# Packed attention and a two-layer sMeLU block on one core: values loaded ahead of queries, head groups by halves, the last output tile in two PSUM tiles, and other planner constants

## The chip, the cores and the metric

The kernel runs on one NeuronCore of a Trainium2 chip. Its time is the device time of one execution in microseconds (us); the figure given is the median over runs. The profile is of one execution and shows what each engine did: TensorE (PE, and PEld for its weight loads), VectorE (DVE), ScalarE (ACT), GpSimd (POOL) and SyncE (SP).

## The reference, cut to what matters

There are 8 batches, 8 heads, 576 tokens of 64 channels, and 32 packing queries per head. All inputs and the output are float32.

```python
p_packed = sm_attn(p, k, v)            # per batch and head: 32 x 64
out = sm_attn(q, p_packed, p_packed)   # 576 x 64
x = out.transpose(0, 2, 1, 3).reshape(8 * 576, 512)
h = x @ w_in                           # 512 -> 2048
g = where(h >= 1, h, where(h <= -1, 0, (h + 1)**2 / 4))
return g @ w_out                       # 2048 -> 512
```

## The kernel before, in words

**The work of a batch.** k and q of a batch are turned so that the channels lie on the partitions (`trans`, line 350): 12 PE transposes for each half of the heads into one PSUM tile, and then a copy to `kT` or `qT`. From batch 3 on (`TURNED`, line 19) DMA transposes on SP's queue do this instead (`turned`, line 485). `scores` (376) multiplies k by the packing queries, 12 matmuls and one exponential on ACT for each half i of the heads. `packed` (397) multiplies by v and sums; three small steps on ACT and DVE make `ppT`, the packed values of each head. The heads are in two groups g of four, and a group's 4 x 32 packed rows fill the 128 rows of a matmul: `weights` (432) makes scores of q against the packed values (`s2`), an exponential `eT`, its sums (`sm`), and by a logarithm and an exponential (`ln`, `rc`) the normalised weights `A`. `mk` (472) multiplies the packed values by a quarter f of w_in (`mp`), which a copy turns into `M`. Both `s2` and `mp` use PE in tiles of 64 rows by 32 columns, eight matmuls at a time; everything else uses the whole array.

**The two layers.** `hidden_tile` (512) makes one of 16 tiles of h of a batch from M and A (4 matmuls), then a first step on ACT, a second on ACT or DVE and a third on DVE, which writes `hT`. `out_tile` (555) sums 16 matmuls ("o-steps", one for each hidden tile) into a PSUM tile `o` for 128 tokens, nine tiles for two batches; then the tile is copied to SBUF (`ob`) and written by SP.

**What sets the order.** `Plan` (31 to 172) is a list scheduler that runs when the program is built. Each task has engines, a cost from the table `C` (line 12), a key and dependences. `choose` (71) takes for each engine the task that can start first, a lower key going ahead; copies that either ACT or DVE may do go to the one that ends sooner. Its order is then the fixed order of each engine's instructions. Until three `o` tiles have been taken it fills PE's idle time with matmuls on zeros (127 to 133 and 624), whose number is fixed by the plan too. PSUM holds three wide tiles ("W", `psW`) and two `o` tiles ("O"). `sc`, `tp`, `s2`, `sm`, `mp` and `h` all take a wide tile.

**Loads.** All loads that cast go through POOL's queue in the order of lines 285 to 299: k of batch 0 in two halves, q, v, then the quarters of w_in and w_out in turn, k, q and v of batch 1, and the rest of p. Loads of batch b + 2 wait until the buffers of batch b have been read (607 to 611). Out writes and DMA transposes stand in SP's queue in the plan's order.

**What the change touches:** the table `C` (12 to 16), `Plan.run` (138 to 142), the first loads (285 to 292), `trans` (366 to 374), `scores`, the head numbers in `packed`, `weights` and `mk`, the last tile in `out_tile` (570 to 585), and the order of keys (602).

Of the kernel before, what the change touches and what calls it, by code (L numbers as in the profile page):

```python
# [8 lines left out]

C = dict(load=3.0, w_in=2.65, w_out=2.55, out=9.0, p=3.1, land=1.9, xt=5.0, xland=2.5,
         tpp=0.06, tp=0.042, sc=0.034, pk=1.05, s2=0.25, sm=0.245, M=0.345, h=0.49, o=0.217, switch=0.05,
         pTc=0.1, Tca=1.12, Tcd=0.76, Tc2a=0.64, Tc2d=0.457, ex=0.82, ppT=0.42, ppo=0.41, ppa=0.4, ppd=0.2, rs=0.18, eT=0.74, ln=0.65, rc=0.68, A=0.82,
         Mca=1.0, Mcd=1.22, x=0.65, ta=0.683, td=0.457, hT=0.758, oba=0.585, obd=0.69,
         array=0.2, wake=2.0, tell=0.04, feed=0.1, slack=0.6, margin=0.15, wait=0.5)
NW, NO, NX, NB = 3, 2, 5, 6
# [13 lines left out]
class Plan:  # L31
# [77 lines left out]
    def run(self, idle):  # L109
# [11 lines left out]
        while n:  # L121
# [54 lines left out]
def kernel(  # L176
# [92 lines left out]

    L = {}  # L270

    def add_load(nm, b, parts=1, deps=()):
        for i, hs in enumerate([ALL] if parts == 1 else HS):
            L[nm, b, i] = add(DMA, C["load"] / parts, -1, deps, lambda nm=nm, b=b, hs=hs: load(nm, b, hs))
        if parts == 1:
            L[nm, b, 1] = L[nm, b, 0]

# [59 lines left out]

    K = {}

    def attention(b, key):  # L340

        kT, qT = lambda: kTs[b % 2], lambda: qTs[b % 2]
# [7 lines left out]
        def trans(nm, i, dst, prev):  # L350
            box, ky = {}, key[nm + "T" + str(i)]

            def mm():
                tp = box["tp"] = wide([P, X, 1024], bf16, "tp")
                for j in range(X):
                    for h2 in range(2):
                        for e in range(E):
                            o = (h2 * E + e) * TP
                            nc.tensor.transpose(tp[:, j, o:o + TP],  # L359
                                                tok[nm, b][:, 4 * i + 2 * j + h2, X * e:X * (e + 1)].rearrange("p c d -> p (c d)"),  # L360
                                                ident[:TP, :TP])
            split = 2 if b == 0 else 1
            t = add(PE, C["tp"] * 12, ky, [L[nm, b, i]] + prev, mm, takes="W", readers=split, mode=0)
            if split == 1:
                def cp(eng):
                    w = 4 * E * TP
                    copy(dst()[:, i, :w].rearrange("p (j c) -> p j c", j=X), box["tp"][:, :, :w // 2])(eng)
                return t, [both(cp, C["Tca"], C["Tcd"], ky, [t], frees=t)]
            res = []
            for j in range(X):  # L370
                def cp(eng, j=j):
                    w = 2 * E * TP
                    copy(dst()[:, i, j * w:(j + 1) * w], box["tp"][:, j, :w])(eng)
                res.append(both(cp, C["Tc2a"], C["Tc2d"], ky, [t], frees=t))
            return t, res

        def scores(i, deps):
            box, ky = {}, key["sc" + str(i)]

            def mm():  # L380
                sp = box["sp"] = wide([P, 2, FW], f32, "sp")
                for j in range(2):
                    for e in range(E):
                        for g in range(G):
                            h, o = G * (2 * i + j) + g, (e * G + g) * X * NP
                            w = ((G * j + g) * E + e) * TP
                            nc.tensor.matmul(sp[:, j, o:o + X * NP], kT()[:, i, w:w + P],  # L387
                                             pT[:, b, h].rearrange("p x n -> p (x n)"), start=True, stop=True)

            def ev(eng):  # L390
                nc.scalar.activation(ex().rearrange("p e g x a n -> p a (e g x) n")[:, 2 * i:2 * i + 2],  # L391
                                     box["sp"][:TP, :, :E * G * X * NP].rearrange("p j (c n) -> p j c n", n=NP),
                                     AF.Exp, scale=scale)
            t = add(PE, C["sc"] * 12, ky, deps, mm, takes="W", readers=1, mode=0)
            return t, add(ACT, C["ex"], ky, [t] + old("pk"), ev, frees=t)

        def packed(deps):
            box, ky = {}, key["pk"]

            def mm():  # L400
                pk = wide([P, 1024], f32, "pk")
                vt, ex_ = tok["v", b], ex()
                v_ = box["v"] = pk[:, :H * X * NP].rearrange("p (h y) -> p h y", h=H)
                for g in range(G):
                    for a in range(Q):
                        h = G * a + g
                        for e in range(E):
                            nc.tensor.matmul(v_[:, h].rearrange("p (x n) -> p x n", x=X),  # L408
                                             vt[:, h, X * e:X * (e + 1)].rearrange("p c d -> p (c d)"), ex_[:, e, g, :, a],
                                             start=(e == 0), stop=(e == E - 1))  # L410
# [21 lines left out]
        def weights(g, deps, r):  # L432
            box, ky, km = {}, key["s2" + str(g)], key["sm" + str(g)]

            def mm():
                s2 = box["s2"] = wide([P, X, FW], f32, "s2")
                for a in range(Q):
                    for x in range(X):
                        nc.tensor.matmul(s2[a * NP:(a + 1) * NP, x, :HALF], pp_of(x, G * a + g),  # L439
                                         qT()[x * D:(x + 1) * D, a // 2, (G * (a % 2) + g) * E * TP:][:, :E * TP], start=True, stop=True)  # L440

            def exp2(eng):
                box["eT"] = att.tile([P, X, HALF], bf16, tag="eT", name="eT")
# [28 lines left out]
        def mk(f, deps):  # L472
            box, ky = {}, key["M" + str(f)]

            def mm():
                mp = box["mp"] = wide([P, G, FW], f32, "mp")
                for a in range(Q):
                    for g in range(G):
                        nc.tensor.matmul(mp[a * NP:(a + 1) * NP, g], pp_of(g, G * a + g),  # L479
                                         w_in_sb[g * D:(g + 1) * D, a, f * FW:(f + 1) * FW], start=True, stop=True)  # L480
            t = add(PE, C["M"], ky, deps + [L["in", f]], mm, takes="W", readers=1, mode=2)
            return t, both(lambda eng: copy(M()[:, :, f * FW:(f + 1) * FW], box["mp"])(eng),
                           C["Mca"], C["Mcd"], ky, [t] + K.get((b - 2, "h"), []), frees=t)

        def turned(nm, i, dst, prev):
            def go():
# [68 lines left out]
    def out_tile(pr, i):  # L555
        box, prev = {}, []
        bs = range(2 * pr + i * P // S, 2 * pr + ((i + 1) * P - 1) // S + 1)

        def step(fi):
            if fi == 0:  # L560
                box["o"] = psO.tile([P, d_model], f32, tag="o", name="o")
            nc.tensor.matmul(box["o"], hT[:, fi, i * P:(i + 1) * P], w_out_sb[:, fi, :], start=(fi == 0), stop=(fi == KF - 1))  # L562

        def done(eng):
            box["ob"] = ops.tile([P, d_model], f32, tag="ob", name="ob")
# [3 lines left out]

        def done_last(eng):  # L570

            w = d_model // 2
            for j, (eng, queue) in enumerate(((ACT, nc.scalar), (DVE, nc.sync))):
                ob = ops.tile([P, w], f32, tag="ob" + str(j), name="ob" + str(j), bufs=1)
                copy(ob, box["o"][:, j * w:(j + 1) * w])(eng)
                for a, n, dst in out_rows(pr, i):
                    queue.dma_start(dst[:, j * w:(j + 1) * w], ob[a:a + n])
        for fi in range(KF):
            t = add(PE, C["o"], 100 + pr * NT + i, [wrote[b, fi] for b in bs] + prev + [L["out", fi // 4]],
                    lambda fi=fi: step(fi), mode=0, takes="O" if fi == 0 else None, readers=1, slack=C["slack"])  # L580
# [1 line left out]
            prev = [t]  # L582
            if fi == 0:
                owner = t
        both(done if 2 * pr + 2 < B or i + 1 < NT else done_last, C["oba"], C["obd"], b_key(pr, i), prev, frees=owner, takes="ob", holds=C["out"])

    def b_key(pr, i):
        return -0.5
# [66 lines left out]
```

## Time and profile before

| what | value |
|---|---|
| median of the runs | 260.59 us (259.56 to 261.15, 3 runs) |
| profiled execution | 259.97 us, of which its span is 258.1 us |
| PE busy | 248.6 us (96%) |
| ACT busy | 189.5 us (73%) |
| DVE busy | 176.1 us (68%) |
| DMA, mean | 133 GB/s, 34.38 MB |

An engine is busy while an instruction is in it. PE's matmuls overlap, so PE at 96% may still lose time; how far apart the starts of equal matmuls lie tells more. The profile's lines name an instruction by its line in the kernel, its engine and its tiles (out<-in). In the timeline a bracket gives the idle time before an instruction and what ended it. In the chain of waits the work that ended last is followed back in time.

### The profile page before, as it was taken

What the parts mean: (1) busy time and instruction counts of PE and PEld (TensorE: products, weight loads), DVE (VectorE), ACT (ScalarE), POOL (GpSimd) and SP (SyncE); (2) the same over time, 40 slices, a digit from 0 to 9 for tenths busy, and PEclk for the clock granted to TensorE, in tenths of its full rate; (3) what the DMA queues carried; (4) which work ended last, traced back from release to release, by engine and by line L of the source; (5) the groups of instructions that cost most, each with busy time, mean ns of one, the idle gap of its engine ahead of it and who ended that gap; (6) DMA issues with size and microseconds to landing.
All of it is one profiled execution on the core that took longest, in us unless ns stands there. A gap on an engine that the chain in (4) does not pass through costs nothing.

```text
span 258.1 us, 5590 instructions
## 1 busy us (share of the span) xinstructions
PE 248.6 (96%) x2273; PEld 145.2 (56%) x2273; DVE 176.1 (68%) x298; ACT 189.5 (73%) x304; POOL 27.4 (11%) x40
## 2 busy tenths in 40 slices
PE   7999999899999999999999999999999999999992
PEld 5977556357646645654655556555654465644440
DVE  5124997678899988999858885888367877940000
ACT  3438995789899799989869987998669885841110
POOL 8522312102101201110201000000000000000000
PEclk9999999999999999999999999999999999999998
DMA  7999999999999999999999994312021111132223
GB/s 100 181 207 207 206 205 194 218 228 209 164 177 165 164 218 195 166 156 144 181 138 159 214 221 89 79 30 54 4 80 41 43 41 42 43 81 82 60 64 83
DMA packets 54762, 34.38 MB, mean 133 GB/s; under 512 B 27472, under 2 KB 50256, under 8 KB 54736
## 3 DMA queue, kind: packets, MB, share of 16 engines
q0 software_dynamic: 24608, 18.55, 51.0%
q1 hardware_dynamic: 29968, 15.34, 33.8%
q8 instruction: 18, 0.29, 0.4%
q10 hardware_dynamic: 160, 0.13, 0.2%
q14 instruction: 8, 0.07, 0.1%
HBM read 37.22 MB, written 9.44 MB: 181 GB/s over the span
## 4 chain that ended last, share of the span: by engine, by line
PE 76%; DMA 15%; ACT 3%; POOL 2%; issue 1%; DVE 1%; POOLq 0%
PE o L562 45%; PE h L519 21%; DMA p_nat<-in_p_dram 8%; DMA w_out_sb<-in_moe_w_out_dram 7%; PE mp L479 3%; PE sp L387 2%; PE pk L408 2%; PE sm L449 1%; PE s L439 1%; ACT M L307 1%; PE tp L359 1%; PE pk L414 1%; ACT pT L307 1%; POOL w_in_sb L280 1%; ACT eT L444 1%
## 5 line engine op out<-in xcount | busy, mean ns | idle before, releaser
L562 PE MATMUL o<-w_out_sb,hT 128*128 128x512 bf16 x576 | 144.5, 379 | 0.7 <-ACT ob L307 0.5
L534 DVE SCALAR_TENSOR_TENSOR hT<-x 128x576 bf16<-128x576 f32 x128 | 93.3, 754 | 14.0 <-PE o L562 9.8
L562 PEld LDWEIGHTS <-hT 128*128 128x128 bf16 x576 | 54.5, 98 | 56.4 <-issue 5.0
L524 ACT ACTIVATE x<-h 128x576 f32<-128x576 f32 x128 | 78.4, 656 | 9.9 <-PE h L519 6.6
L519 PE MATMUL h<-A,M 128*128 128x288 bf16 x512 | 77.8, 286 | 0.3 <-ACT M L307 0.3
L519 PEld LDWEIGHTS <-M 128*128 128x128 bf16 x512 | 48.4, 98 | 24.7 <-issue 3.0
L529 DVE TENSOR_SCALAR x<-x 128x576 f32<-128x576 f32 x80 | 36.7, 459 | 16.9 <-ACT x L524 16.2
L307 ACT COPY ob<-o 128x512 f32<-128x512 f32 (+1 forms) x22 | 12.7, 577 | 30.8 <-PE o L562 30.7
L531 ACT ACTIVATE x<-x 128x576 f32<-128x576 f32 x48 | 32.1, 683 | 0.7
L307 DVE COPY ob<-o 128x512 f32<-128x512 f32 (+1 forms) x15 | 10.1, 673 | 26.6 <-ACT ob L307 24.9
L307 ACT CAST M<-mp 128x1024 bf16<-128x1024 f32 x20 | 19.9, 1008 | 1.2 <-PE mp L479 1.1
L624 PE MATMUL o<-zeros 128*128 128x256 bf16 x137 | 18.9, 285 | 1.2 <-DVE zeros L242 1.2
L307 DVE CAST M<-mp 128x1024 bf16<-128x1024 f32 x12 | 14.6, 1220 | 1.7 <-PE mp L479 1.6
L624 PEld LDWEIGHTS <-zeros 128*128 128x128 bf16 x137 | 13.4, 102 | 3.5 <-DVE zeros L242 1.2
L460 DVE SCALAR_TENSOR_TENSOR A<-eT,rs,rc 128x576 bf16<-128x576 bf16 x16 | 13.0, 814 | 2.7 <-ACT rc L457 2.6
L391 ACT ACTIVATE ex<-sp 96x768 bf16<-96x768 f32 x16 | 12.9, 814 | 2.0 <-PE sp L387 2.0
L254 POOL DMA_DIRECT2D k<-in_k_dram x9 | 7.3, 812 | 65.9 <-issue 28.0
L444 ACT ACTIVATE eT<-s,rs 128x576 bf16<-128x576 f32 x16 | 11.7, 743 | 2.9 <-PE s L439 2.8
L479 PE MATMUL mp<-w_in_sb,ppT 64*32 64x512 bf16 x256 | 13.1, 384 | 0.5 <-ACT x L524 0.5
L453 ACT ACTIVATE ln<-sm 128x576 f32<-128x576 f32 x16 | 10.5, 655 | 1.6 <-PE sm L449 1.4
L457 ACT ACTIVATE rc<-ln 128x576 f32<-128x576 f32 x16 | 10.9, 683 | 0.5
L387 PEld LDWEIGHTS <-kT 128*128 128x128 bf16 x192 | 7.8, 98 | 2.2 <-ACT kT L307 0.2
(47 smaller groups left out, 114.1 us busy)
## 6 DMA issues: line engine op xcount, KB each, us to landing
q<-in_q_dram POOLq DMA_DIRECT2D x8, 576.0 KB, 14.5
v<-in_v_dram POOLq DMA_DIRECT2D x8, 576.0 KB, 15.0
out_dram<-ob SPq DMA_DIRECT2D x23, 192.0 KB, 3.0
k<-in_k_dram POOLq DMA_DIRECT2D x7, 576.0 KB, 14.1
out_dram<-ob SPq DMA_DIRECT2D x24, 128.0 KB, 2.4
w_in_sb<-in_moe_w_in_dram POOLq DMA_DIRECT2D x4, 512.0 KB, 18.3
w_out_sb<-in_moe_w_out_dram POOLq DMA_DIRECT2D x4, 512.0 KB, 19.0
out_dram<-ob SPq DMA_DIRECT2D x23, 64.0 KB, 2.6
```

The source lines that it names most:

```text
L307: return lambda eng: nc.vector.tensor_copy(out_, in_) if eng == DVE else nc.scalar.copy(out_, in_)
L387: nc.tensor.matmul(sp[:, j, o:o + X * NP], kT()[:, i, w:w + P], pT[:, b, h].rearrange("p x n -> p (x n)"), start=True, stop=True)
L444: nc.scalar.activation(box["eT"], box["s2"][:, :, :HALF], AF.Exp, scale=rs()[:, g, 1:])
L460: nc.vector.scalar_tensor_tensor(A()[:, g], box["eT"], rs()[:, g, :1], box["rc"], ALU.mult, ALU.mult)
L479: nc.tensor.matmul(mp[a * NP:(a + 1) * NP, g], pp_of(g, G * a + g), w_in_sb[g * D:(g + 1) * D, a, f * FW:(f + 1) * FW], start=True, stop=True)
L519: nc.tensor.matmul(h[:, hf, :HALF], T[b, "M"][:, g, fi * P:(fi + 1) * P], T[b, "A"][:, g, hf], start=(g == 0), stop=(g == G - 1))
L524: nc.scalar.activation(box["x"], box["h"][:, :, :HALF], AF.Prelu, bias=-1.0, alpha=0.5)
L529: nc.vector.tensor_scalar(x, x, 1.0, 0.0, ALU.add, ALU.max)
L531: nc.scalar.activation(x, x, AF.Relu, bias=1.0)
L534: nc.vector.scalar_tensor_tensor(hT[:, fi, col:col + S].rearrange("p (a t) -> p a t", a=2), box["x"], 1.0, box["x"], ALU.min, ALU.mult)
L562: nc.tensor.matmul(box["o"], hT[:, fi, i * P:(i + 1) * P], w_out_sb[:, fi, :], start=(fi == 0), stop=(fi == KF - 1))
L624: plan.run(lambda: nc.tensor.matmul(o[:, :DW], zeros[:, :P], zeros[:, :DW], start=True, stop=True))
```

## The change

- The loads of batch 0 stand as k (two halves), v, q (two halves); before they stood as k (two halves), q, v.
- Head groups: `head(g, a) = 4 g + (a ^ g)`. Group 0 holds heads 0 to 3 and group 1 holds heads 5, 4, 7, 6; before, group g held the heads 2a + g. So `scores(i)` makes the exponentials of group i alone, and the `s2` of a group needs one half of qT alone. In `mk` the row half of PE is now that of the head's parity, no longer that of the group.
- `trans` copies a half of the heads in one piece for batch 0 too, on one engine; before, DVE and ACT copied half of it each.
- The first copy of M is DVE's.
- The last output tile sums its 512 columns as two of 256 in two PSUM tiles (the second a wide one), and each engine copies one; its larger rows are written first.
- The plan: `xland`, the landing of a DMA transpose after its issue, 6.0 for 2.5; a step of ACT or DVE of over 0.4 gives the engine back 0.085 sooner (`lap`); a switch of PE's mode is counted at 0.09 and only into the tiled mode (before 0.05, both ways); the first v and q are counted at 3.8 (`first`).

```diff
-         tpp=0.06, tp=0.042, sc=0.034, pk=1.05, s2=0.25, sm=0.245, M=0.345, h=0.49, o=0.217, switch=0.05,
+         tpp=0.06, tp=0.042, sc=0.034, pk=1.05, s2=0.25, sm=0.245, M=0.345, h=0.49, o=0.217, switch=0.09, lap=0.085, join=0.11,
...
-                cost += C["switch"]
+                cost += C["switch"] if t.mode else 0.0
...
-            self.now[e] = at + cost
+            self.now[e] = at + cost - (C["lap"] if e in ("ACT", "DVE") and cost > 0.4 else 0.0)
...
+        load("v", 0, ALL)
         make_identity(nc, ident)
...
-    add_load("q", 0)
-    add_load("v", 0)
+    L["v", 0, 0] = L["v", 0, 1] = add(DMA, C["first"], -1, (), lambda: None)
+    add_load("q", 0, 2, cost="first")
...
+    def head(g, a):
+        return 4 * g + (a ^ g)
...
-                sp = box["sp"] = wide([P, 2, FW], f32, "sp")
-                for j in range(2):
-                    for e in range(E):
-                        for g in range(G):
-                            h, o = G * (2 * i + j) + g, (e * G + g) * X * NP
-                            w = ((G * j + g) * E + e) * TP
-                            nc.tensor.matmul(sp[:, j, o:o + X * NP], kT()[:, i, w:w + P],
-                                             pT[:, b, h].rearrange("p x n -> p (x n)"), start=True, stop=True)
+                sp = wide([P, 1024], f32, "sp")
+                box["sp"] = sp[:TP, :E * X * Q * NP].rearrange("p (e y) -> p e y", e=E)
+                for e in range(E):
+                    o = sp[:, e * X * Q * NP:(e + 1) * X * Q * NP].rearrange("p (x a n) -> p x a n", x=X, a=Q)
+                    for a in range(Q):
+                        h = head(i, a)
+                        w = (h % 4 * E + e) * TP
+                        nc.tensor.matmul(o[:, :, a], kT()[:, i, w:w + P], pT[:, b, h], start=True, stop=True)
...
-                        nc.tensor.matmul(mp[a * NP:(a + 1) * NP, g], pp_of(g, G * a + g),
-                                         w_in_sb[g * D:(g + 1) * D, a, f * FW:(f + 1) * FW], start=True, stop=True)
+                        h = head(g, a)
+                        y = h % 2
+                        nc.tensor.matmul(mp[a * NP:(a + 1) * NP, g], pp_of(y, h),
+                                         w_in_sb[y * D:(y + 1) * D, h // 2, f * FW:(f + 1) * FW], start=True, stop=True)
...
+            if (b, f) == (0, 0):
+                return t, add(DVE, C["Mcd"], ky, [t], cp, frees=t)
...
-        ws = [weights(g, pc + qc0 + qc1, r) for g in range(G)]
+        ws = [weights(g, pc + (qc0, qc1)[g], r) for g in range(G)]
...
-            nc.tensor.matmul(box["o"], hT[:, fi, i * P:(i + 1) * P], w_out_sb[:, fi, :], start=(fi == 0), stop=(fi == KF - 1))
+            for o, cs in [(box["o"][:, :w], slice(w)), (box["o2"], slice(w, d_model))] if end else [(box["o"], slice(d_model))]:
+                nc.tensor.matmul(o, hT[:, fi, i * P:(i + 1) * P], w_out_sb[:, fi, cs], start=(fi == 0), stop=(fi == KF - 1))
...
-            for j, (eng, queue) in enumerate(((ACT, nc.scalar), (DVE, nc.sync))):
+            for j, (eng, queue, o) in enumerate(((ACT, nc.scalar, box["o"][:, :w]), (DVE, nc.sync, box["o2"]))):
...
-                copy(ob, box["o"][:, j * w:(j + 1) * w])(eng)
-                for a, n, dst in out_rows(pr, i):
+                copy(ob, o)(eng)
+                for a, n, dst in sorted(out_rows(pr, i), key=lambda x: -x[1]):
...
-    order = "kT0 qT0 kT1 sc0 qT1 sc1 pk s20 M0 s21 sm0 M1 sm1 M2 M3".split()
+    order = "kT0 kT1 sc0 qT0 sc1 qT1 pk s20 M0 s21 sm0 M1 sm1 M2 M3".split()
```

More of the change, by code (lines that the diff above doesn't have):

```diff
@@ L8 @@
 from concourse._compat import with_exitstack
-C = dict(load=3.0, w_in=2.65, w_out=2.55, out=9.0, p=3.1, land=1.9, xt=5.0, xland=2.5,
-         tpp=0.06, tp=0.042, sc=0.034, pk=1.05, s2=0.25, sm=0.245, M=0.345, h=0.49, o=0.217, switch=0.05,
-         pTc=0.1, Tca=1.12, Tcd=0.76, Tc2a=0.64, Tc2d=0.457, ex=0.82, ppT=0.42, ppo=0.41, ppa=0.4, ppd=0.2, rs=0.18, eT=0.74, ln=0.65, rc=0.68, A=0.82,
+C = dict(load=3.0, first=3.8, w_in=2.65, w_out=2.55, out=9.0, p=3.1, land=1.9, xt=5.0, xland=6.0,
+         tpp=0.06, tp=0.042, sc=0.034, pk=1.05, s2=0.25, sm=0.245, M=0.345, h=0.49, o=0.217, switch=0.09, lap=0.085, join=0.11,
+         pTc=0.1, Tca=1.12, Tcd=0.76, ex=0.82, ppT=0.42, ppo=0.41, ppa=0.4, ppd=0.2, rs=0.18, eT=0.74, ln=0.65, rc=0.68, A=0.82,
          Mca=1.0, Mcd=1.22, x=0.65, ta=0.683, td=0.457, hT=0.758, oba=0.585, obd=0.69,
@@ L361, in mm, with cp @@
                                                 ident[:TP, :TP])
[L362 to L375, printed above, removed]
+            t = add(PE, C["tp"] * 12, ky, [L[nm, b, i]] + prev, mm, takes="W", readers=1, mode=0)
+            def cp(eng):
+                w = 4 * E * TP
+                copy(dst()[:, i, :w].rearrange("p (j c) -> p j c", j=X), box["tp"][:, :, :w // 2])(eng)
+            return t, [both(cp, C["Tca"], C["Tcd"], ky, [t], frees=t)]
         def scores(i, deps):
@@ L557, in out_tile, with spare @@
         bs = range(2 * pr + i * P // S, 2 * pr + ((i + 1) * P - 1) // S + 1)
+        end = 2 * pr + 2 == B and i + 1 == NT
+        w = d_model // 2
+        def spare():
+            box["o2"] = wide([P, w], f32, "o2")
         def step(fi):
@@ L584, in out_tile @@
                 owner = t
-        both(done if 2 * pr + 2 < B or i + 1 < NT else done_last, C["oba"], C["obd"], b_key(pr, i), prev, frees=owner, takes="ob", holds=C["out"])
+        both(done_last if end else done, C["oba"], C["obd"], b_key(pr, i), prev, frees=owner, takes="ob", holds=C["out"])
     def b_key(pr, i):
```

23 lines of the change are left out of this document (12 added, 11 removed).

## The prediction

> **What bounds the kernel now.** I read the windows by stage first, then the chain of waits, then the timeline where PE is not full.
>
> ```profile
> span 258.1 us, 5590 instructions
> 0.00:23.60 23.60, 21.57 (x277) 17.70 (x277) 8.78 (x24) 10.18 (x16) 11.63 (x21) 1.00 1.11 170
> 23.60:82.00 58.40, 55.66 (x607) 33.39 (x600) 48.16 (x78) 50.65 (x80) 8.59 (x11) 1.00 1.33 198
> 82.00:223.60 141.60, 141.60 (x1262) 80.77 (x1260) 113.71 (x189) 120.48 (x195) 7.19 (x9) 1.00 0.76 116
> 223.81 29.58 PE o L562 x137
> 20.36 3.00 PE L624 MATMUL o<-zeros 128*128 128x256 bf16 x26
> ```
>
> The second number after the length is PE's busy time. From 82 to 223.6 us PE is never idle, and then 137 o-steps run at 29.58 / 137 = 0.216 us each; a tile of h takes 0.49 (a chain row below has eight h matmuls in 0.98). So after 82 us there is nothing to gain but at the very end: the change must win before 82 us, and what it puts off there costs in full. Before 23.6 us PE mostly turns zeros, (3.00 - 0.27) / 25 = 0.11 us each.
>
> ```profile
> 11.75 0.75 POOL L280 DMA_DIRECT2D w_in_sb<-in_moe_w_in_dram  x1 [2.42 <-DMA q<-in_q_dram]
> 15.63 0.87 PE L408 MATMUL pk<-ex,v 96*128 96x64 bf16 x24 [0.36 <-DMA v<-in_v_dram]
> 22.71 0.82 DVE L460 SCALAR_TENSOR_TENSOR A<-eT,rs,rc 128x576 bf16<-128x576 bf16 x1 [0.58 <-ACT rc L457]
> 23.64 1.15 PE L519 MATMUL h<-A,M 128*128 128x288 bf16 x8
> 26.04 0.65 PE L519 MATMUL h<-A,M 128*128 128x288 bf16 x4
> 33.10 0.11 PEld L479 LDWEIGHTS <-ppT 64*32 64x32 bf16 x8 [0.29 <-DMA w_in_sb<-in_moe_w_in_dram]
> 34.54 0.99 ACT L307 CAST M<-mp 128x1024 bf16<-128x1024 f32 x1
> 35.68 2.12 PE L519 MATMUL h<-A,M 128*128 128x288 bf16 x16
> 38.52 1.19 PE L359 MATMUL tp<-ident,k 96*128 96x96 bf16 x24 [0.50 <-DMA k<-in_k_dram]
> 44.36 0.87 PE L408 MATMUL pk<-ex,v 96*128 96x64 bf16 x24 [0.38 <-DMA v<-in_v_dram]
> 47.01 0.81 PE L562 MATMUL o<-w_out_sb,hT 128*128 128x512 bf16 x3 [0.46 <-ACT ob L307]
> 50.20 0.41 PE L449 MATMUL sm<-eT,onesblk 128*128 128x288 bf16 x2 [0.27 <-ACT pT L307]
> 55.47 0.65 PE L519 MATMUL h<-A,M 128*128 128x288 bf16 x4
> 76.94 0.41 PE L479 MATMUL mp<-w_in_sb,ppT 64*32 64x512 bf16 x8 [0.53 <-ACT x L524]
> 79.30 0.65 PE L519 MATMUL h<-A,M 128*128 128x288 bf16 x4 [0.27 <-ACT M L307]
> ```
>
> The third load is in SBUF by 11.7, the fourth by 15.6; batch 0's A waits for it and the first h runs at 23.64. But the stream of loads goes on: the last quarter of w_in stops PE at 33.1, k of batch 1 at 38.5, its v at 44.36. These loads keep their places. The brackets from 38.5 on sum to 0.50 + 0.38 + 0.46 + 0.27 + 0.53 + 0.27 = 2.4 us: about all that a better order could still find.
>
> **The change, part by part.** I walk through the order in which the changed program is built, each step beginning at the latest of its data, its engine and its PSUM tile, with these durations:
>
> ```profile
> L307 DVE COPY kT<-tp 128x1152 bf16<-128x1152 bf16 x2 | 1.4, 753 | 0.5 <-PE tp L359 0.5
> L307 ACT COPY kT<-tp 128x1152 bf16<-128x1152 bf16 x2 | 2.2, 1112 | 0.0
> L307 DVE COPY ob<-o 128x512 f32<-128x512 f32 x14 | 9.7, 691 | 1.7 <-PE o L562 1.2
> L453 ACT ACTIVATE ln<-sm 128x576 f32<-128x576 f32 x16 | 10.5, 655 | 1.6 <-PE sm L449 1.4
> L457 ACT ACTIVATE rc<-ln 128x576 f32<-128x576 f32 x16 | 10.9, 683 | 0.5
> 24.69 3.92 ACT L524 ACTIVATE x<-h 128x576 f32<-128x576 f32 x7
> 38.51 1.28 ACT L531 ACTIVATE x<-x 128x576 f32<-128x576 f32 x2
> ```
>
> *Loads, whole copies, groups by halves.* The copies of a half in batch 0 become one of 0.753 on DVE; they end before v lands either way, so this costs and gains nothing. v now lands third, by 11.7; pk stands behind 15 zeros, which end at 12.65, where it started at 15.63. The halves of q land at about 13.7 (halfway between the third and the fourth load) and 15.6. With 7 zeros, the transposes and a copy, qT's first half is ready at 15.9, and 11 zeros end at 16.1: s2 of group 0 runs at 16.2. Group 1 follows its half of q: transposes at 16.55, copy to 18.0, s2 at 18.25, its sm behind the first M block at 19.85; ln, rc and A (0.655 + 0.683 + 0.82, with the steps between) end at 22.5, and 24 zeros at 22.7. First h at 22.7: 0.9 us sooner.
>
> *What becomes of it by 44 us.* The second M block now stands behind three tiles of h, and its copy on ACT behind three first steps (3.92 / 7 = 0.56 each): it ends at 26.1, h tile 4 starts at 26.45 (before 26.04), and two o-steps more are done. The fourth M block comes after four h tiles and five o-steps, and its copy after two extra second steps on ACT (0.64 each): 35.3 to 36.3 (before 34.54 to 35.53). h tile 12 is at 36.45 (before 35.68) with three o-steps (0.65) more: all of the 0.9 is gone. Four o-steps then stand ahead of k's transposes: 39.45 (before 38.52). The first copy of kT falls to ACT, behind two second steps: 40.6 to 41.7, where DVE took 0.75 at once. The next o tile needs the first one's copy by DVE (0.691): 43.7 to 44.4. Six o-steps stand ahead of pk, so pk is at 45.8 (before 44.36), with 38 o-steps ahead of it instead of 30: 8 x 0.216 = 1.73 done for 1.44 us. Ahead by 0.3.
>
> *Batch 1's attention.*
>
> ```profile
> 47.77 0.79 ACT L307 COPY pT<-tpp 64x768 bf16<-64x768 bf16 x1 [0.39 <-DVE pT L307]
> 48.59 0.56 DVE L307 COPY pT<-tpp 64x768 bf16<-64x768 bf16 x1 [0.86 <-ACT pT L307]
> 49.35 0.79 ACT L307 COPY pT<-tpp 64x768 bf16<-64x768 bf16 x1
> 56.13 0.51 PE tp L359 x12
> ```
>
> The four copies from one PSUM tile go one after the other. Now three are ACT's: 3 x 0.79 + 0.55 from 47.35 end at 50.2 with the steps between. The s2 of group 1 takes their PSUM tile (the built addresses say so) and stops PE from 49.3 to 50.35. Both orders have 57 o-steps ahead of batch 1's first h. It comes at 56.65 (before 55.47), with one more group of transposes (0.51) done: behind by 0.7.
>
> *Batch 1's h, batch 2's attention.*
>
> ```profile
> 65.90:78.21 12.31, 11.77 (x135) 6.21 (x134) 11.18 (x20) 11.32 (x19) 0.77 (x1) 1.00 1.36 178
> 80.16 0.98 PE h L519 x8
> ```
>
> Here ACT is the limit (11.32 of 12.31 us), as the waits at 76.94 and 79.30 say. pk goes ahead of two h tiles, which leaves seven tiles and 19 o-steps to cover the chain of s2, sm and A instead of four and 15. But the second M copy of this batch moves from DVE to ACT, 1.0 us on the engine that is late. Step by step h tile 0 of batch 2 comes at 79.45 instead of 78.21, with the same work ahead (90 o-steps); some of the 1.2 comes back in the next waits: 1.1 us behind at 81.4.
>
> *After 82 us.* Earlier sc and pk mean fewer o-steps as cover: between batch 3's first h and batch 4's s2 stand 7 o-steps, where 23 stood. Each of the eleven tiles of h there asks 0.56 of ACT and 0.49 of PE, so ACT falls up to 11 x 0.07 = 0.8 behind. Bounds: 0 (no wait shows in this stage now) and 16 x 0.216 = 3.5 us (all of the lost cover missed); I take 0.4, near the lower, as half of those 0.8. DMA transposes:
>
> ```profile
> 62.66 5.89 SPq L487 DMA_TRANSPOSE qT<-q  x1
> ```
>
> Both of k now stand ahead of both of q on SP (before, q's first stood between), so sc's second half has its data one issue (5.89 us) sooner, while 20 o-steps fewer (4.3 us) stand ahead of it in batch 4. SP's outputs stand between them; I cost this at nothing, covered by that issue, and at up to 4 us if a write that waits for its copy holds it up. The plan's 6.0, lap and switch act through the order alone; both orders enter the tiled mode 40 times.
>
> *The end.*
>
> ```profile
> 253.41 0.37 ACT L307 COPY ob<-o 128x256 f32<-128x256 f32 x1 [2.82 <-PE o L562]
> 253.82 0.86 ACTq L577 DMA_DIRECT2D out_dram<-ob  x2
> 253.82 0.42 DVE L307 COPY ob<-o 128x256 f32<-128x256 f32 x1 [24.86 <-ACT ob L307]
> 254.27 0.82 SPq L577 DMA_DIRECT2D out_dram<-ob  x2
> ```
>
> DVE waited for ACT's copy from the same PSUM tile; from its own it starts 0.41 sooner. The larger write, issued second, ended last; issued first it goes half of 0.82 sooner, and the smaller one then ends last, which I estimate to leave 0.2 of that. Two matmuls of 256 columns cost 32 x 0.11 - 16 x 0.216 = 0.06. Together -0.6.
>
> *Sum:* +1.1 + 0.4 - 0.6 = +0.9 us on the profiled execution, which has 259.97 us (span 258.1 and 1.9 around it), 0.6 under the median. On the median: 260.59 + 0.9 = 261.5.
>
> **A row against a rule.** The M block of the changed kernel sends both row halves of PE into each of its two PSUM banks; before, each half had a bank.
>
> ```profile
> 52.38 0.34 PE mp L479 x8
> ```
>
> Eight matmuls of 512 columns take 0.34 us in all, one alone 0.216: they overlap. The Trainium skill (TensorEngine Tiling (Array Packing), Gotcha 1: PSUM Pressure) says that different row tiles cannot access one PSUM bank at the same time. By that rule the halves would take turns; no row here shows it, and the sum above takes nothing. [...]
>
> **The rivals.**
> 1. *Faster.* The plan's order holds better than my walk: the six waits of 2.4 us go, as they are what the new lap and the earlier pk address, and the end gives 0.6: 260.59 - 3.0 = 257.6, over 1% under. For it: seven tiles cover batch 2's chain. Against: ACT is full there. It decides if ACT, not PE, has idle time in 66 to 78 us.
> 2. *Slower by lost cover.* One mechanism, 82 to 130 us: with 16 o-steps fewer before batch 4's s2, PE stands while ACT catches up. It costs 3.5 us at most; with the rest, 260.59 + 1.1 + 3.5 - 0.6 = 264.6. It decides from about 2.1 us of waits there (263.2 in all). Against it: PE's row of 141.60 in 141.60 leaves room unseen.
> 3. *Slower by turns in a bank.* If the row halves take turns, each of 32 M blocks is two rounds, 0.216 more: +6.9, so 268.4. Nothing in before bears on it, as each half has its own bank there.
> 4. *It does nothing:* the sooner h is eaten by the loads, nothing else moves: 260.0. This lies within my forecast's own range.
>
> **How the numbers follow.** My walk (with rival 4): 0.60, own range 260.0 to 263.0; rival 1: 0.15; rival 2: 0.20; rival 3: 0.05. The range leaves out rival 3 and most of rival 1: 258.3 to 264.6. A change of under 1% (2.6 us) can hardly be told from none here: within it falls the walk, 0.60; faster 0.15; slower 0.20 + 0.05 = 0.25.
>
> **What would show it.** First h near 22.7; pk of batch 1 near 45.8; a wait of about 1 us of s2 for pT near 50; first h of batch 2 near 79.5; PE full from 82 on but for a few tenths; M blocks of 0.34; both last copies starting together. I am wrong if batch 2's first h comes before 78, if PE shows waits of over 1 us after 82, or if M blocks lengthen.

## The result and the profile after

The changed kernel takes 262.01 us (median of 9 runs, 261.55 to 264.05), the kernel before 259.74 (9 runs, 259.28 to 261.15): a ratio of 1.0102, 95% interval 1.0079 to 1.0125. The forecast was 261.5 against 260.59, a ratio of 1.0035; the time lies in its range. So much for the sum. The terms behind it are another matter: up to batch 2 the change gained 1.5 us where I had it losing, and behind that it lost about 3.4 us where I had it losing 0.4. (Three runs, one of the kernel before and two of kernels below, were over 1% longer at a granted clock of 0.946 to 0.993 and are left out.)

The windows of the profiled execution after, then the last of them for the kernel before and for the changed kernel without `lap` (the first experiment). The numbers in brackets are instructions; the second bracket counts weight loads, one for each matmul.

```profile
span 259.8 us, 5588 instructions
0.00:22.50 22.50, 20.90 (x266) 17.28 (x267) 10.06 (x24) 7.93 (x12) 11.81 (x22) 1.00 1.10 171
22.50:82.00 59.50, 56.16 (x621) 34.53 (x630) 47.02 (x81) 52.99 (x82) 10.07 (x12) 1.00 1.30 204
82.00:222.00 140.00, 137.75 (x1199) 77.62 (x1219) 105.11 (x186) 113.10 (x184) 6.35 (x8) 1.00 0.71 112
```

```profile
82.00:222.00 140.00, 140.00 (x1250) 79.56 (x1248) 112.22 (x186) 118.88 (x192) 7.19 (x9) 1.00 0.77 117
```

```profile
82.00:222.00 140.00, 138.39 (x1218) 79.90 (x1239) 114.31 (x187) 117.13 (x193) 6.64 (x8) 1.00 0.72 115
```

In the same 140 us PE began 1219 matmuls instead of 1248. (PE's busy time is no guide here: the two traces with 1199 and 1218 matmuls miss about 20 records each, which leaves holes in it; the loads are all there.) Which ones are missing is in the groups of weight loads by line in that stretch: M is the operand of h, hT that of an o-step, kT that of the scores. First before, then after.

```profile
L519 PEld LDWEIGHTS <-M 128*128 128x128 bf16 x355 | 33.7, 98 | 17.2 <-issue 1.3 <-PE s L439 1.0
L562 PEld LDWEIGHTS <-hT 128*128 128x128 bf16 x345 | 32.8, 98 | 31.3 <-issue 2.8
L387 PEld LDWEIGHTS <-kT 128*128 128x128 bf16 x108 | 4.4, 98 | 1.1
```

```profile
L522 PEld LDWEIGHTS <-M 128*128 128x128 bf16 x345 | 32.8, 97 | 18.2 <-issue 3.6
L572 PEld LDWEIGHTS <-hT 128*128 128x128 bf16 x338 | 32.2, 98 | 32.3 <-issue 4.0
L387 PEld LDWEIGHTS <-kT 128*128 128x128 bf16 x96 | 3.9, 98 | 0.9
```

A matmul of h is worth 0.49 / 4 = 0.1225 us, an o-step 0.216, one of the scores 0.03 (12 in 0.35). So 10 x 0.1225 + 7 x 0.216 + 12 x 0.03 = 3.1 us of work were not done. I call this the work lost behind 82 us; it is counted, not read from idle time.

PE's timeline of the kernel after, with the places that the forecast named, and ACT's at the one wait among them:

```profile
22.52 1.63 PE L522 MATMUL h<-A,M 128*128 128x288 bf16 x12
33.95 0.41 PE L479 MATMUL mp<-w_in_sb,ppT 64*32 64x512 bf16 x8
34.30 1.04 PE L572 MATMUL o<-w_out_sb,hT 128*128 128x512 bf16 x4
35.88 2.13 PE L522 MATMUL h<-A,M 128*128 128x288 bf16 x16 [0.55 <-ACT M L309]
45.08 0.86 PE L405 MATMUL pk<-ex,v 96*128 96x64 bf16 x24
49.72 0.32 PE L437 MATMUL s<-qT,ppT 64*32 64x288 bf16 x8 [1.60 <-ACT pT L309]
55.44 0.65 PE L522 MATMUL h<-A,M 128*128 128x288 bf16 x4
76.22 1.29 PE L522 MATMUL h<-A,M 128*128 128x288 bf16 x8
```

```profile
46.65 1.60 ACT L309 COPY pT<-tpp 64x768 bf16<-64x768 bf16 x2
48.87 0.79 ACT L309 COPY pT<-tpp 64x768 bf16<-64x768 bf16 x1 [0.62 <-DVE pT L309]
```

The first h is where I put it (22.52; forecast 22.7), and s2 of group 1 does wait for the copies of pT, for 1.60 us rather than the 1 forecast. But h tile 12 is at 35.88 (36.45), pk at 45.08 (45.8), batch 1's first h at 55.44 (56.65), and batch 2's first h is the second tile of the row at 76.22, so at 76.71 (79.45; before 78.21, with the same 90 o-steps ahead). The M block still takes 34.30 - 33.95 = 0.35 us.

The last copies of the kernel after:

```profile
255.30 0.37 ACT L309 COPY ob<-o 128x256 f32<-128x256 f32 x1 [2.75 <-PE o L572]
255.41 0.42 DVE L309 COPY ob<-o 128x256 f32<-128x256 f32 x1 [25.60 <-PE o L572]
255.71 0.86 ACTq L586 DMA_DIRECT2D out_dram<-ob  x2
255.86 0.79 SPq L586 DMA_DIRECT2D out_dram<-ob  x2
```

They start together, as the edit means them to. From the first copy to the end of the span it is 259.8 - 255.30 = 4.5 us, and was 258.1 - 253.41 = 4.7: the end is worth 0.2.

So the profiled pair, 259.8 - 258.1 = +1.7, is -1.5 by batch 2's first h, about +3.4 behind it (3.1 of it in the counted 140 us), and -0.2 at the end. Both executions start alike: the 28 zeros from 4.41 us on take 2.99 us in each, which matters below.

### The profile page after: what moved, and what is told of

Read it like the earlier page. It is cut to its first block, busy times and chain, and to the rows that moved or that the text cites. A ratio compares the mean times of both kernels' runs of the same rounds, so it can differ in the third digit from the quotient of the medians.

```text
span 259.8 us, 5588 instructions
## 1 busy us (share of the span) xinstructions
PE 248.0 (95%) x2253; PEld 146.3 (56%) x2287; DVE 170.2 (66%) x302; ACT 184.9 (71%) x296; POOL 28.2 (11%) x41
## 4 chain that ended last, share of the span: by engine, by line
PE 73%; ACT 15%; DVE 7%; issue 3%; ACTq 0%
PE o L572 38%; PE h L522 21%; ACT x L527 6%; PE o L635 5%; DVE hT L537 4%; PE mp L479 3%; ACT M L309 2%; ACT x L534 2%; PE sp L387 2%; ACT eT L442 2%; ACT ln L451 1%; PE s L437 1%; PE tp L366 1%; PE pk L405 1%; DVE x L532 1%
## 5 line engine op out<-in xcount | busy, mean ns | idle before, releaser
L572 PE MATMUL o<-w_out_sb,hT 128*128 128x512 bf16 (+1 forms) x558 | 133.1, 373 | 1.3 <-issue 0.5
L572 PEld LDWEIGHTS <-hT 128*128 128x128 bf16 x592 | 56.0, 98 | 55.9 <-issue 5.4
L532 DVE TENSOR_SCALAR x<-x 128x576 f32<-128x576 f32 x92 | 41.3, 457 | 12.3 <-ACT x L527 11.8
L309 ACT CAST M<-mp 128x1024 bf16<-128x1024 f32 x29 | 29.1, 1015 | 0.0
L534 ACT ACTIVATE x<-x 128x576 f32<-128x576 f32 x36 | 24.0, 685 | 0.6
L635 PE MATMUL o<-zeros 128*128 128x256 bf16 x135 | 18.2, 285 | 1.2 <-DVE zeros L243 1.2
L255 POOL DMA_DIRECT2D q<-in_q_dram x9 | 7.1, 794 | 30.3 <-DMA qT<-q 19.5
```

The lines of the kernel that those rows point to most:

```text
L255: nc.gpsimd.dma_start(tok[nm, b][:, hs].rearrange("p h c d -> p h (c d)"), SRC[nm][b, hs].rearrange("h (p c) d -> p h (c d)", c=NC))
L309: return lambda eng: nc.vector.tensor_copy(out_, in_) if eng == DVE else nc.scalar.copy(out_, in_)
L532: nc.vector.tensor_scalar(x, x, 1.0, 0.0, ALU.add, ALU.max)
L534: nc.scalar.activation(x, x, AF.Relu, bias=1.0)
L572: nc.tensor.matmul(o, hT[:, fi, i * P:(i + 1) * P], w_out_sb[:, fi, cs], start=(fi == 0), stop=(fi == KF - 1))
L635: plan.run(lambda: nc.tensor.matmul(o[:, :DW], zeros[:, :P], zeros[:, :DW], start=True, stop=True))
```

## The experiments

**Which part costs: the plan's credit, or the rest?** The first four kernels take the change apart. Without the credit alone:

```diff
-         ... switch=0.09, lap=0.085, join=0.11,
+         ... switch=0.09, lap=0.0, join=0.11,
```

> The changed kernel with lap 0 instead of 0.085, so that the plan again counts each ACT and DVE step in full. Theory A (the lap lets the plan set tiles of h so close that PE waits for ACT by some hundredths at each, 3.3 us in all after 82 us): the waits after 82 us fall back to about those of before, PE is full there, and the time comes to about 257.5 to 259, 3 to 4 under the changed kernel and 1 to 2 under before. Theory B (the groups by halves and the other structure cost the time after 82 us, whatever the plan counts): 261 to 262, as the changed kernel.

Measured: 256.9 us (256.75 to 257.81), against 259.94 for the kernel before on the same chip: ratio 0.9891 (0.9869 to 0.9914). One number in the plan, which changes no step but only the order of the steps and which of ACT and DVE does a copy, is worth 5.1 us, and without it the change is a gain of 3 us. The groups of loads from 82 to 222 us say where:

```profile
L522 PEld LDWEIGHTS <-M 128*128 128x128 bf16 x356 | 33.8, 98 | 18.5 <-issue 2.8 <-PE h L522 0.2
L572 PEld LDWEIGHTS <-hT 128*128 128x128 bf16 x347 | 33.0, 98 | 30.5 <-issue 2.5
L387 PEld LDWEIGHTS <-kT 128*128 128x128 bf16 x96 | 3.9, 98 | 0.8
```

11 matmuls of h and 9 o-steps more than after in the same time: 1.35 + 1.94 = 3.3 us. The rest of the 4.9 us between the spans (259.8 and 254.9), 1.6 us, was lost before 82. There the 1.60 us that s2 waits for the copies of pT are gone without the credit: PE's waits from 28 to 82 us sum to about 3.0 us after, 1.3 without the credit and 2.7 before.

The same with the other two numbers of the plan put back as well:

```diff
-         ... xt=5.0, xland=6.0,
+         ... xt=5.0, xland=2.5,
-         ... switch=0.09, lap=0.085
+         ... switch=0.05, lap=0.0
-                cost += C["switch"] if t.mode else 0.0
+                cost += C["switch"]
```

> The changed kernel with all planner constants as before (lap 0, landing 2.5, switch 0.05 both ways): loads, halves, whole copies, first M copy and last tile alone. Theory A: as with lap 0 alone, 257.5 to 259. Theory B: 261 to 262. Theory C (the later landing is needed now that scores are asked for sooner): a wait for DMA transposes of over 1 us shows on PE between 100 and 130 us, which lap 0 alone doesn't have.

Measured: 257.49 us (257.0 to 258.09), ratio 0.9904 (0.9884 to 0.9924). PE shows no wait for a DMA transpose between 100 and 130 us, so theory C falls. The landing time of the DMA transposes and the price of the switch do nothing that shows beside `lap`.

The credit alone, on the kernel before:

```diff
-            self.now[e] = at + cost
+            self.now[e] = at + cost - (C["lap"] if e in ("ACT", "DVE") and cost > 0.4 else 0.0)
```

> The kernel before with the lap of 0.085 alone. Theory A: it has 64 pairs of h tiles with nothing between them on PE, where before has 42 and the changed kernel 48; waits of PE for ACT after 82 us of 3 to 5 us, and a time of 262 to 264. Theory B: the lap does nothing by itself, 259.5 to 260.5.

Measured: 263.95 us (263.08 to 264.2), ratio 1.0144 (1.0122 to 1.0166): 4.0 us slower. So the credit costs with either structure, 4.0 on the old one and 5.1 on the new one, and the other parts gain 3.0 without it and 1.9 with it.

The end alone, on the kernel before (two PSUM tiles for the last tile, the larger write first):

```diff
-                copy(ob, box["o"][:, j * w:(j + 1) * w])(eng)
-                for a, n, dst in out_rows(pr, i):
+                copy(ob, o)(eng)
+                for a, n, dst in sorted(out_rows(pr, i), key=lambda x: -x[1]):
```

> The kernel before with the last output tile in two PSUM tiles and its larger rows first, nothing else; the order of the rest is the same. The forecast's term of the sum: both copies start together and the last landing is 0.5 to 0.6 sooner, 259.2. Rival: the writes' own time sets the end, whichever copy comes first, 259.7.

Measured: 259.88 us, ratio 0.9996 (0.9984 to 1.0009). The two copies do start together in this kernel's timeline:

```profile
253.76 0.37 ACT L307 COPY ob<-o 128x256 f32<-128x256 f32 x1 [2.75 <-PE o L569]
253.87 0.42 DVE L307 COPY ob<-o 128x256 f32<-128x256 f32 x1 [24.50 <-PE o L569]
```

From the first copy to the end of the span (258.2) it is 4.4 us, 0.3 less than before. The edit does what it says, and is worth half of the 0.6 forecast at most; the runs can't tell it from nothing.

**Where does the credit cost?** The next two kernels give it to one half of the time each; the condition is on the time at which the plan places the step.

```diff
-... (C["lap"] if e in ("ACT", "DVE") and cost > 0.4 else 0.0)
+... (C["lap"] if e in ("ACT", "DVE") and cost > 0.4 and at > 82.0 else 0.0)
```

> The changed kernel, but the plan takes the 0.085 us of overlap into account only for steps that it places after 82 us. Without it the kernel took 256.9, with it 262.0: 5.1 us. Theory A (the credit lets ACT look as fast as PE, so fewer o-steps stand between tiles of h and PE waits): the lost starts of PE are 2.0 us more before 82 (4.90 against 2.93) and 3.4 us more behind it (1.87 + 2.78 against 0.27 + 0.98), so this kernel takes 256.9 + 3.4 = 260.3, and shows PE waiting behind 82 as the changed kernel does. Rival B (what is lost behind 82 is only the wait that an earlier stage passes on): 257 to 257.5. Rival C (any other order is as bad as any, the differences are chance): somewhere between 257 and 262 without waits behind 82.

> The changed kernel, with the 0.085 us of overlap only for steps that the plan places up to 82 us. Theory A: it loses the 2.0 us before 82 alone, above all the wait of s2 for the PSUM tile of pT near 50 us, and shows PE full from 82 on: 256.9 + 2.0 = 258.9. Rival B (the early part is what matters): 261 to 262. Rival C (as for the kernel before this one): between 257 and 262.

The second has `at <= 82.0`. Measured: 260.91 us with the credit behind 82 alone (ratio 1.0039, 1.0023 to 1.0055), 259.03 with the credit before 82 alone (0.9974, 0.9951 to 0.9998). Expected were 260.3 and 258.9; rival C asked for no waits behind 82 in the first, and there they are. The loads from 82 to 222 us, the late credit first:

```profile
L522 PEld LDWEIGHTS <-M 128*128 128x128 bf16 x352 | 33.4, 97 | 18.4 <-issue 3.2
L572 PEld LDWEIGHTS <-hT 128*128 128x128 bf16 x331 | 31.5, 98 | 31.7 <-issue 3.8
```

```profile
L522 PEld LDWEIGHTS <-M 128*128 128x128 bf16 x356 | 33.9, 98 | 18.3 <-issue 2.1
L572 PEld LDWEIGHTS <-hT 128*128 128x128 bf16 x347 | 33.0, 98 | 30.9 <-issue 3.1
```

With the late credit 4 matmuls of h and 16 o-steps are missing against the kernel without it: 0.5 + 3.5 = 4.0 us. With the early one none: it loses before 82 what it loses and nothing behind. But not all that it loses is the credit's. In its profiled execution the first h comes at 23.69 instead of 22.63, since the zeros at the start took longer (more on this below); of the 257.4 - 254.9 = 2.5 us between the spans that leaves about 1.4 for the early credit. With 3.8 (258.7 - 254.9) for the late one this makes 5.2, near the 4.9 of both together. The wait of 1.6 us of s2 for pT is back in the second kernel and absent in the first. So the places are shown, and the larger part is the one behind 82.

How PE loses the time shows in a single wait of the kernel after, whose tile of h starts 0.05 us after a first step of ACT has ended:

```profile
106.22 0.65 ACT L527 ACTIVATE x<-h 128x576 f32<-128x576 f32 x1
106.92 0.65 PE L522 MATMUL h<-A,M 128*128 128x288 bf16 x4 [0.30 <-ACT x L527]
```

Most of these waits are too short to leave PE idle in the profile. I count them from start to start, with 0.1225 us for a matmul of h and 0.216 for an o-step. Behind 82 us, 28 tiles of h begin late and 0.05 us after such a step, by about 2.5 us in all. With the late credit alone there are 27 (2.1 us); without the credit 3 (0.3), with the early credit alone 3 (0.1), and in the kernel before 1 (0.03). These waits are the larger part of the 3.1 us of work lost. In the kernel before with the credit alone there are 15 (0.9 us), and other tiles of h there wait for DVE, so on the old structure this is only a part.

The last tiles of h, where no other work is mixed in, show the pace. PE and ACT of the kernel after, then PE of the kernel before:

```profile
219.90 3.44 ACT L527 ACTIVATE x<-h 128x576 f32<-128x576 f32 x6
220.59 3.45 PE L522 MATMUL h<-A,M 128*128 128x288 bf16 x24
223.88 31.50 PE L572 MATMUL o<-w_out_sb,hT 128*128 128x512 bf16 x158
```

```profile
222.66 1.14 PE L519 MATMUL h<-A,M 128*128 128x288 bf16 x8
223.64 29.73 PE L562 MATMUL o<-w_out_sb,hT 128*128 128x512 bf16 x137
```

After, six tiles of h stand in a row and take (223.88 - 220.59) / 6 = 0.55 us each, the pace of ACT's first steps beside them (3.44 / 6 = 0.57). Before, two stand in a row between o-steps, at 0.49 each: PE's own pace. PE can begin a tile of h only when one of the three wide PSUM tiles has been emptied, in such a row by ACT. The credit is right as a fact: of six first steps in 3.44 us, five take (3.44 - 0.656) / 5 = 0.557, 0.10 less than one alone (0.656, the mean of the 128 in the kernel before). The Trainium skill (ScalarE: Activation LUTs, What ACT_TABLE_LOAD costs) has 93 ns for the overlap of such steps, and the trace agrees. But an ACT at 0.56 to 0.57 is still slower than PE at 0.49. The plan puts an o-step ahead of a tile of h only where it sees that tile wait by more than half an o-step (`choose`); with the credit it sees less of the wait and leaves the o-steps for later. They do not go away: behind the last h stand 161 loads of o-steps instead of 137, of which 16 are the second halves of the last tile's, so 8 o-steps more. The late credit alone has 161 too; without the credit, and with the early one alone, there are 153, as many as before with the 16. Behind the last h nothing is left that they could cover.

The copies of M go the same way. These are the groups of ACT in the same stretch, after and then without the credit:

```profile
L309 ACT CAST M<-mp 128x1024 bf16<-128x1024 f32 x19 | 19.1, 1014 | 0.0
```

```profile
L309 ACT CAST M<-mp 128x1024 bf16<-128x1024 f32 x10 | 10.1, 1005 | 0.0
```

With the credit the plan finds room on ACT for nine more copies of 1.0 us. None of the 28 waits ends with such a copy; how much of ACT's lateness in them is these copies' doing is not separated.

**Is the plan without the credit at its best, or would more caution help?** Here the sign is turned round (`lap=-0.03`, so each such step counts 0.03 longer).

> The changed kernel with the credit turned round: the plan makes every step of ACT and DVE over 0.4 us 0.03 us longer for the next one instead of 0.085 shorter. Theory A (what counts is that the plan does not overrate ACT): PE stays full behind 82 us, so as without the credit, 256 to 257.5. Rival L (the plan without the credit is at its best by luck, any step from it costs): 258 or more.

> The changed kernel without the credit once more, as the base for the three kernels run beside it. All theories: 256.9, as before. If it comes out 1 us or more away, the differences of 1 us between kernels of different calls can't be read.

Measured: 258.59 us turned round (ratio 0.9949, 0.9932 to 0.9966), 257.18 without credit (0.9897, 0.9882 to 0.9911). More caution costs 1.4 us, so rival L holds and A's simple form does not: what is overrated costs, but so does what is underrated. By the loads about 1.0 us of it is lost from 30 to 82 us (3 matmuls of h and 3 o-steps less) and 0.5 behind (4 o-steps less, 3 matmuls of h more), without a wait of h for ACT's first steps there; the cause stays open. So a small change of this constant can cost 1 us or more by another way; the 28 waits and the 5 us are the credit's.

**Which of the other parts gain the 3 us?** The next four kernels start from the changed kernel without the credit. The loads of batch 0 as keys, queries, values, once with the identity behind both loads of the queries and once behind the first:

```diff
-        load("v", 0, ALL)
+        load("q", 0, HS[0])
+        load("q", 0, HS[1])
         make_identity(nc, ident)
```

> The changed kernel without the credit (256.9), and with the loads of batch 0 again in the order keys, queries, values; all else of the change stays. My forecast gave the load order 0.9 us at the first h and nothing of it by 44 us. Theory D (the 0.9 us at the first h is kept to the end as long as the plan keeps PE covered): 256.9 + 0.9 = 257.8, first h near 23.5. Rival E (it is eaten by the later loads, as forecast, and the gain comes from the order of the later batches and whole copies): 256.9.

> As the run with the queries loaded first, but with the identity built behind the first of the queries' loads, so that it is there as soon as in the changed kernel. In the run before this one the identity came 0.9 us later, the zeros on TensorE then ran at half pace for longer, and the first scores came 2.42 us later than in the kernel without the credit; at the end PE was 3.36 us behind it. Theory D (the load order itself is worth its 0.9 us at the first h, kept to the end): 256.9 + 0.9 = 257.8, first scores again near 9.5, first h near 23.5 to 24. Rival E (the load order is worth the whole 3.2 us): 260.1 again. Rival H (nothing but the late identity cost time): 256.9.

Measured: 260.09 us (258.08 to 261.08; ratio 0.9999, 0.9976 to 1.0022) and 259.6 (257.62 to 260.91; ratio 0.9977, 0.9953 to 1.0002), so 2.4 us or more slower than the kernel without the credit (the base), where 0.9 was expected. Both medians come with wide spreads, and the profiles say why part of it is no matter of the order. Here are the weight loads of the first zeros, for the kernel without the credit, the first of these two, and the kernel with the old order of batches (below):

```profile
4.41 2.99 PEld L635 LDWEIGHTS <-zeros 128*128 128x128 bf16 x28
```

```profile
4.89 4.92 PEld L637 LDWEIGHTS <-zeros 128*128 128x128 bf16 x28
```

```profile
4.42 4.21 PEld L635 LDWEIGHTS <-zeros 128*128 128x128 bf16 x28
```

The same 28 zeros take 2.99 us or 4.92 and end 2.4 us later. In the first of the two orders the cause of a part is its own: the transposes of p waited for the identity, and their loads and the zeros behind them began 0.5 us later (the 0.9 in the expectation is the whole idle time there). In the last of the three kernels nothing in the program differs up to there, and the zeros end 1.2 us late. So the start moves a profiled execution by 1.2 us with no cause in the program, and by 2.4 where the identity comes late as well. In the second of the two orders the zeros end only 0.2 us late; its span is 256.2 us, 1.3 over the base's 254.9, and its first h is the row at 24.62, the base's the one at 22.63:

```profile
24.62 1.15 PE L524 MATMUL h<-A,M 128*128 128x288 bf16 x8
```

```profile
22.63 1.63 PE L522 MATMUL h<-A,M 128*128 128x288 bf16 x12
```

By this one profile, then, the load order is worth 2.0 - 0.2 = 1.8 us at the first h, of which 1.3 - 0.2 = 1.1 are left at the end: about theory D's size. The median, 2.4 us over the base, is nearer to E's. Why it is 1.6 us over its own profiled execution (257.96) stays open, since only that one has a trace; the start alone could do it.

The s2 of group 0 waiting for both halves of q again:

```diff
-        ws = [weights(g, pc + (qc0, qc1)[g], r) for g in range(G)]
+        ws = [weights(g, pc + qc0 + qc1, r) for g in range(G)]
```

> The changed kernel without the credit, but the s2 of group 0 waits for both halves of q again. In the changed kernel group 0's s2 stood at 16.2 and group 1's at 18.2, and A of group 1 set the first h. Theory J (the groups by halves let ln, rc and A of group 0 run before those of group 1; without that the two follow each other on ACT): first h some 0.5 to 1.0 us later, 257.4 to 257.9. Rival K (group 1 sets the first h either way): first h near 22.5, 256.9.

Measured: 260.21 us (257.92 to 261.48; ratio 1.0009, 0.9981 to 1.0036). More than any theory had. The profile has two pieces of it, PE's first h and a wait in batch 3's attention:

```profile
24.18 1.63 PE L522 MATMUL h<-A,M 128*128 128x288 bf16 x12
92.11 0.32 PE L437 MATMUL s<-qT,ppT 64*32 64x288 bf16 x8 [1.53 <-DMA qT<-q]
```

The first h comes 24.18 - 22.63 = 1.55 us later, 0.5 of it from the zeros, so 1.1 from the halves: J's end of the range and a little over. The other 1.5 us are a DMA transpose that lands late. It is the term that I had costed at nothing and bounded by 4; here it shows for once, in a kernel that the forecast was not about. Whether the edit makes it late or this one execution did is open; the spread of the runs is 3.6 us.

The order of the steps of batches 1 to 7 put back:

```diff
-    order = "kT0 kT1 sc0 qT0 sc1 qT1 pk s20 M0 s21 sm0 M1 sm1 M2 M3".split()
+    order = "kT0 qT0 kT1 sc0 qT1 sc1 pk s20 M0 s21 sm0 M1 sm1 M2 M3".split()
```

> The changed kernel without the credit (256.9), and with the keys of batches 1 to 7 in the old order, kT0 qT0 kT1 sc0 qT1 sc1, instead of kT0 kT1 sc0 qT0 sc1 qT1. In the built program 44 pairs of h tiles then follow each other with nothing between, as in the kernel before (42), against 32. Theory F (the new order of batch b+1's transposes and scores is what saves the waits between 28 and 82 us, 5.52 against 2.93): 259 to 259.5. Rival G (it saves nothing; pairs as in the kernel before cost nothing there either, 1.31 us behind 82): 256.9 to 257.5.

Measured: 258.58 us (258.19 to 258.99; ratio 0.9945, 0.9928 to 0.9963), 1.4 to 1.7 over the base. It lies between F and G. In its profile the zeros ended 1.2 us late, and the span is 2.3 over the base's, which leaves about 1.1 us for the order. So the load order (1.1), the halves (1.1 at the first h) and the order of the batches (about 1.1) each carry a part of the gain; none is the gain. Each of these sizes is from one execution, with its start taken off. In medians putting the three back costs 2.4, 3.0 and 1.4 us, together more than twice the gain of 3.0, so the medians don't settle how it is divided.

The kernel without the credit, at 256.9 and 257.18 us in two sets of runs, is the fastest of all that ran and beats both kernels by 1% or more.

## Why the prediction came out right, and where it was wrong

*Right:* the first h at 22.7 (22.52); the wait of s2 for the PSUM tile of pT; M blocks unchanged, which refutes rival 3; no wait of PE for a DMA transpose in the changed kernel; the last copies together. Of the three signs that I had named for being wrong, the M blocks' did not come; the other two did.

*Wrong, first:* "1.1 us behind at 81.4". Measured is 1.5 us ahead at batch 2's first h, where I had written 79.45 and the row says 76.71. I had said that I'd be wrong if it came before 78. The walk added the waits behind ACT's queue one by one, each from steps of full length, and was too late by 0.6 at h tile 12, by 0.7 at pk, by 1.2 at batch 1's first h and by 2.7 at batch 2's. The larger error is in the last stretch, where I let the M copy on ACT cost 1.0 and had "ACT is the limit". Here is that stretch, from batch 1's first h to batch 2's, before and then after (the third busy time is DVE's, the fourth ACT's):

```profile
55.47:78.21 22.74, 22.20 (x258) 13.94 (x257) 19.57 (x34) 20.84 (x32) 2.58 (x3) 1.00 1.33 187
```

```profile
55.44:76.71 21.27, 20.93 (x242) 13.39 (x245) 19.17 (x34) 20.92 (x33) 2.51 (x3) 1.00 1.29 200
```

ACT was the limit, but it was idle for 1.9 us there before and for 0.35 after. With one instruction more it fills the idle time that the walk had left standing. I had also let the sooner first h be all gone by h tile 12. With the o-steps done ahead counted (3 more there, 8 more at pk), the kernel was 0.65 - 0.20 = 0.45 us ahead at h tile 12 and 1.73 - 0.72 = 1.0 ahead at pk. Rival 1 had the sign of this part, but not its way: ACT has no idle time to speak of after, and PE's waits from 28 to 82 us, which it took off, are 3.0 us after against 2.7 before. They fall (to 1.3) only without the credit.

*Wrong, second:* "I take 0.4, near the lower". The term behind 82 us was about 3.4, at the upper bound of 3.5 that I had given for rival 2, to which I had given a chance of 0.20. Its size was right, and so was its mechanism, PE standing while ACT catches up (the 28 waits). Its place was only half right: it had the loss between 82 and 130 us, where batch 4's s2 has less cover. By the count of loads used above, 1.4 of the 3.1 us are lost up to 125 us and 1.7 behind it, up to the last tiles of h. I had written that "the plan's 6.0, lap and switch act through the order alone", and then priced the order by one place in it. Of these three numbers `lap` alone made the order cost 5 us.

*Wrong, third:* the end, -0.6 forecast, -0.2 in the profile and at most -0.3 alone. DVE's copy starts 0.11 us behind ACT's where it was 0.41, so the copies give 0.3 instead of 0.41; of the larger write going first nothing is to be seen, and why stays open.

The forecast of +0.9 thus came from +1.1 + 0.4 - 0.6 where the profile has -1.5 + 3.4 - 0.2. Two errors of 2.6 and 3.0 us with opposite signs made it look good, which is luck; in medians it was +2.3.

On the rule against the row: the Trainium skill (TensorEngine Tiling (Array Packing), Gotcha 1: PSUM Pressure) does not allow different row tiles one PSUM bank at the same time. The M block after, with both row halves in each bank, takes 0.35 us, where it took 0.34 before, so here they do not take turns.

## What to carry to other kernels

When a list scheduler's costs are made truer for one engine, look at what it then stops doing: a credit of 0.085 us to an engine that stays the slower one took the filler from between its steps, and cost 4 to 5 us of 260. Price such a constant by going through the two built orders stage by stage, not by one place that looks thin; afterwards, the count of started work per stage shows where it cost. And where a change joins structure and tuning constants, split the two first: here one gained 3 us, and the other took 5.

## What the runs showed of the hardware

The pace of TensorE at the start is not the same in each execution. A zeros matmul of 256 columns takes 0.107 us (2.99 / 28), but about 0.2 at first (12 loads in 2.26 us). The moment of the change was early in the executions of the kernels before and after. In all profiled executions but that of the kernel with the late identity, PE's instructions are the same up to the end of the 28 zeros, and these took from 2.99 to 4.21 us, with the granted clock at 1.00 in the profile's rows all the while. The Trainium skill (TensorE: Matmul & The Clock Gate, What's actually happening) says that the warm-up is run-variable, as its window is free-running; the traces agree that it varies, and here the 1.2 us are of the size of the differences measured. The window itself no run here shows. A kernel of 260 us that fills its start with zeros should be compared by several runs for differences of 1 us, and by profiles only after a look at the zeros.

One DMA transpose can also take very different times to issue on SP: 1.36 us and 5.33 us in these two rows of one kernel (the one that waits for both halves), with one instruction each.

```profile
100.84 5.33 SPq L490 DMA_TRANSPOSE qT<-q  x1
112.08 1.36 SPq L490 DMA_TRANSPOSE kT<-k  x1
```
